# Two small moves in a long-convolution kernel: which engine copies part of Z out of PSUM, and which queue reads an identity matrix

## The chip, the cores and the metric

The kernel runs on one core of one Trainium2 chip. A core has five engines that run their own instruction streams side by side: TensorE (PE in the profile; its weight loads are listed apart as PEld), VectorE (DVE), ScalarE (ACT), GpSimd (POOL) and SyncE (SP), which only issues transfers here. They wait for each other through semaphores. The metric is device time in microseconds; the time shown is the median of three runs.

## The reference

The input x is 8 batches of 5696 positions and 128 channels. Two steps follow each other. The first is a causal convolution of each channel with a filter h as long as the sequence, done with transforms of twice the length:

```python
Xf = np.fft.rfft(x, n=L, axis=1)          # L = 2 * 5696
Hf = np.fft.rfft(h, n=L, axis=0)
y = np.fft.irfft(Xf * Hf[None], n=L, axis=1)[:, :S, :]
```

The second takes the lowest 64 frequencies of that result, mixes the channels of each with a complex 128x128 matrix, transforms back, adds, and ends with one matrix product:

```python
X = np.fft.rfft(y, axis=1)[:, :64]
Y = complex product of X with w_r + i w_i, mode by mode
u = y + np.fft.irfft(Y padded with zeros, n=S, axis=1)
out = u + np.maximum(u @ w_ch, 0.0)
```

## The kernel before, in words

The batches go in four pairs (`g_` from 0 to `NP - 1` = 3). The sequence is split as 89 x 64, and each transform becomes matrix products in float16. For each pair the kernel first makes the tiles `As` (a transform over the 89), and then runs through 90 frequencies `k` in 23 ticks of four (`ticks`, `KT = 4`), followed by three ticks in which the pipeline empties. The function `tick(g_, t)` writes out one such step, and the order in which it emits instructions is the order on every engine: each engine has one queue, and a recorder adds the semaphore waits that the data need. Helpers issue almost everything, so the profile shows their lines: 323 for a matmul, 311 for a ScalarE copy, 315 for a VectorE copy, 320 for a transfer.

In the last three pairs a tick consists of:

- `second(g_, t)`: 32 matmuls in two ticks (`ps<-As,M`), emitted for t and t + 1 together when t is odd;
- `products(g_, t, ...)`: the product with the filter's spectrum, on VectorE (`U<-Xs,Hs`, line 637). In three ticks of four ScalarE first copies the matmuls' result from PSUM to the tile `Xs`, and VectorE reads that copy. In each tick with t % 4 == 3 (`straight`) VectorE reads PSUM itself (`U<-ps,Hs`);
- for the tick `s_ = t - 2` (`LC = 2`): four matmuls with the matrices W1 and W2 (`ps<-U,Wc`), two for each batch b of the pair, and after each two a copy of the bank to the tile Z (`Zs` or `Zt`, half b). Both copies are on ScalarE. Three PSUM banks take turns for this (`ZBANK`). A transfer on SP's queue then writes Z to DRAM (`zscr<-Zs`);
- for the tick `s_ = t - 3` (`LM = 3`): eight matmuls that read Z as their weights (`ps<-G,Zs`), for each of the four frequencies first b = 0, then b = 1. They gather the 64 low modes.

So on TensorE the order in an odd tick is `As,M`, `U,Wc`, `G,Z`, and in the even tick after it `U,Wc`, `G,Z`. The `G,Z` matmuls of a tick read the Z that was copied in the tick before. On VectorE the order is one product a tick.

In the last pair the list `early` has, at certain ticks, transfers and clearings for the stage that follows: weights, tables, the first chunks of Z read back (`load_zt`) and zeros in 32 rows of them, by GpSimd (`clear_zt`). At tick 14 it calls `load_id()`, `load_ib()` and `clear_zt(1)` in that order. `load_id` reads a 128x128 identity, which is used once, in the eight transposes of Y (line 824) after the pair. Its tile lies where the Z tiles 8 and 9 were, so the transfer waits until those have been read and written out (`ZY`).

After the last pair come the mode mixing, the transposes of Y, and the long last stage, in which 16 chunks of Z are read back and each output tile is made of matmuls, one ScalarE and one VectorE pass and a transfer.

Of the kernel before, what the change touches and what calls it, by code (L numbers as in the profile page):

```python
# [4 lines left out]
P = 128  # L5
# [118 lines left out]
def bass_long_conv_fft__then__afno_spectral_mix_kernel(nc, x, h, moe_w_r, moe_w_i, moe_w_ch, out):  # L124
    B, S, D = x.shape
# [7 lines left out]
    NP = B // 2  # L133
# [17 lines left out]
    c, s = np.cos(th), np.sin(th)  # L151
# [35 lines left out]
    def const(name, a):  # L187
        return nc.inline_tensor(np.ascontiguousarray(a.astype(np.float16)), name=name)
# [3 lines left out]
    c_w = const("cW", np.concatenate([w1, w2, np.eye(P)], axis=1))  # L192
# [5 lines left out]
    zs = nc.dram_tensor("zscr", [NP * NK * P, 2 * D], F16, kind="Internal")  # L198
# [7 lines left out]
    def at(name, cols, dt, off):  # L206
        return nc.alloc_sbuf_tensor_at(name, [P, cols], dt, offset=off)
# [75 lines left out]
    id_sb = at("Id", P, F16, r_off[1])  # L283
# [8 lines left out]
    def pv(bank, off, dims, p0=0, n=P):  # L292
        return bass.AP(ps, p0 * 4096 + bank * 512 + off, [[4096, n]] + [list(d) for d in dims])
# [5 lines left out]
    def bank(i):  # L299
        return ("bank", i)  # L300
# [18 lines left out]
    def dma(eng, dst, src, ring, reads=(), writes=(), after=()):  # L319
        R.add(eng, lambda h_: h_.dma_start(dst, src), reads, writes, ring=ring, after=after)  # L320
# [14 lines left out]
    def turns(name, items):  # L335
        i = ring2.get(name, 0)
        ring2[name] = i + 1
        return items[i % len(items)]
# [25 lines left out]
    def x_place(i, src, toks):  # L364
        R.add("vector", lambda e: e.tensor_copy(bass.AP(x_sb, i * XN * XS, [[XW, NQ], [XS, XN], [1, D]]),  # L365
                                                src),
              list(toks) + XZ, [("xin", i)])
# [72 lines left out]
    for j in range(16):  # L440
        t = turns("h", [0, 2, 4])
# [5 lines left out]
        for i in range(4 if j < 15 else 26):  # L447
# [4 lines left out]
             eng="vector" if j in (3, 7) else "scalar")  # L452
# [25 lines left out]
    def xtok(n):  # L478
        return [("xt", n, p_) for p_ in range(2)]

    def x_room(g_, i):
        if g_ > 1:
            return x_st[i]
        return x_h[i] if i < NXH else x_st[i - NXH]
# [37 lines left out]
    ZY = [("zs", i, b) for i in range(NZL, NZX) for b in range(2)]  # L522
# [42 lines left out]
    pace = []  # L565

    def load_id():
        dma("sync", id_sb[:, :], bass.AP(c_w, 2 * P, [[3 * P, P], [1, P]]), "c", (), [("id",)], after=ZY)

    def load_wi():  # L570
        dma("gpsimd", wi_sb[:, P:2 * P], bass.AP(c_w, 2 * P, [[3 * P, P], [1, P]]), "p", (), [("i16",)], after=M_ALL[5:6])
# [6 lines left out]
    LC, LM, LH = 2, 3, 6  # L578
# [3 lines left out]
    def with_h_at(g_, t):  # L582
        return g_ == 0 and t + LH < NT
# [10 lines left out]
    def twin(g_, t):  # L594
        return g_ > 0 and t % 2 == 1
# [4 lines left out]
    def slot_of(g_, t):  # L600
        if g_ == 0 or t == 0:
            return XSLOT[(t + 1) % 2 if t and not with_h_at(g_, t) else 0]
        return XSLOT[((t - 1) // 4 + t) % 2]

    def second(g_, t):
        sl = slot_of(g_, t)
        for i, k in enumerate(ticks[t]):
            for r in range(2):
                for b in range(2):
                    col = k * 3 * J + (J if r == 0 else 0) + b * J  # L610
                    mm(pv(sl + b, i * D, [[1, D]]),
                       ap(m_sb, MW, J * b, J, col, [[1, P]]),
                       ap(a_sb, AW, J * b, J, (2 * k + r) * D, [[1, D]]), r == 0, r == 1,
                       AST + mtok(k), [bank(sl + b)])

    def products(g_, t, sl):
        n = len(ticks[t])
        bk = [bank(sl), bank(sl + 1)]
        i = t % NU
        hv = bass.AP(h_sb, KT * t * D, [[2 * HW, P], [HW, 2], [0, 2], [1, n * D]])  # L620
        uv = bass.AP(u_s[i], 0, [[2048, P], [1024, 2], [512, 2], [1, n * D]])
        src = pv(sl, 0, [[0, 2], [512, 2], [1, n * D]])
        if t == 0:
            e = turns("e", list(range(NXS)))
            evac(bass.AP(x_s[e], 512, [[1024, P], [1, n * D]]), pv(sl + 1, 0, [[1, n * D]]), [bank(sl + 1)], [("xs", e)], eng="scalar")
            hv = bass.AP(h_sb, 0, [[2 * HW, P], [HW, 2], [1, n * D]])
            for b, s_, tok in ((0, pv(sl, 0, [[0, 2], [1, n * D]]), bank(sl)),
                               (1, bass.AP(x_s[e], 512, [[1024, P], [0, 2], [1, n * D]]), ("xs", e))):
                R.add("vector", lambda e, b=b, s_=s_: e.tensor_tensor(bass.AP(u_s[i], b * 512, [[2048, P], [1024, 2], [1, n * D]]), s_, hv, MULT),  # L629
                      [tok, ("h", t, 0), ("h", t, 1, 0), ("h", t, 1, J)], [("u", i)])  # L630
            return
        if not straight(g_, t):
            e = onchip.get((g_, t))
            if e is None:
                e = copied(g_, t, sl)
            src, bk = bass.AP(x_s[e], 0, [[1024, P], [0, 2], [512, 2], [1, n * D]]), [("xs", e)]
        R.add("vector", lambda e: e.tensor_tensor(uv, src, hv, MULT),  # L637
              bk + [("h", t, 0), ("h", t, 1, 0), ("h", t, 1, J)], [("u", i)])
# [10 lines left out]
    def tick(g_, t):  # L649
        if g_ + 1 < NP:  # L650
            for i in range(2 * XC):
                if t == XPLACE[g_ > 0][i]:
                    x_place(i, bass.AP(x_room(g_ + 1, i), 0, [[XB, NQ], [D, XN], [1, D]]), xtok(i))
        with_h = with_h_at(g_, t)
        if t < NT:
            of_two = t > 0 and twin(g_, t - 1)
            if not of_two:
                second(g_, t)
            products(g_, t, slot_of(g_, t))
            if twin(g_, t):  # L660
                second(g_, t + 1)
                if straight(g_, t):
                    copied(g_, t + 1, slot_of(g_, t + 1))
        drain = list(border[t]) if t in border and g_ + 1 < NP else []
        if drain and t >= NT:
            j, sl, e = drain.pop(0)
            a_tile(j, [sl], e)
        if g_ + 1 < NP:
            i = t // 2 - 1 if t % 2 == 0 else -1
            if g_ == 0:  # L670
                i = XLATE.index(t) + NXH if t in XLATE else -1
            if 0 <= i < 2 * XC:
                x_load(g_ + 1, i, x_room(g_ + 1, i), xtok(i), [("u", t % NU)] + AST)
        if LC <= t < NT + LC:
            s_ = t - LC
            n = len(ticks[s_])
            i, zi = s_ % NU, zroom(g_, s_)
            zb = [turns("z", ZBANK) for b in range(2)]
            for b in range(2):
                for r in range(2):  # L680
                    mm(pv(zb[b], 0, [[1, n * D]]), (W1, W2)[r], u_s[i][:, r * 1024 + b * 512:r * 1024 + b * 512 + n * D],
                       r == 0, r == 1, [("u", i), ("wc",)], [bank(zb[b])])
                evac(bass.AP(z_s[zi], b * D, [[1024, P], [2 * D, n], [1, D]]),
                     pv(zb[b], 0, [[D, n], [1, D]]), [bank(zb[b])], [("zs", zi, b)], eng="scalar",
                     after=once(("zx", zi, b), Z_OLD) if zi >= NZ else ())
            zo = (g_ * NK + KT * s_) * P * 256
            dma("sync", bass.AP(zs, zo, [[256, P], [P * 256, n], [1, 256]]),
                bass.AP(z_s[zi], 0, [[1024, P], [256, n], [1, 256]]), "z",
                [("zs", zi, 0), ("zs", zi, 1)], [("zd", g_, s_)])
            if drain and t >= NT:  # L690
                j, sl, e = drain.pop(0)
                a_tile(j, [sl], e)
        if LM <= t < NT + LM:
            s_ = t - LM
            zi = zroom(g_, s_)
            for i, k in sorted(enumerate(ticks[s_]), key=lambda q: (s_ > 0 or q[1] != 1, q)):
                for b in range(2):
                    if k % 2:
                        o, off, n, sl = pv(MB, b * P, [[1, P]]), (k + 1) // 2 * P, P, (k + 1) // 2
                    else:  # L700
                        ms, off = even[k]
                        n, sl = 2 * len(ms), 0
                        dims = [[M, 2]] if len(ms) == 1 else [[ms[1] - ms[0], 2], [M, 2]]
                        o = pv(MB, b * P + ms[0], dims)
                    mm(o, z_s[zi][:, i * 256 + b * P:i * 256 + b * P + P], g_sb[:, off:off + n],
                       k == 1 and b == 0, k == NK - 1 and b == 1, [("g", sl // GP), ("zs", zi, b)], [bank(MB)])
        if drain and t < NT + LM - 1:
            j, sl, e = drain.pop(0)
            a_tile(j, [sl], e)
        if with_h:  # L710
            filter_tick(t + LH, [2, 3])
# [106 lines left out]
    for hb in range(2):  # L818
        evac(bass.AP(y_sb, hb * 32 * B, [[2 * M * B, P], [B, 32], [M * B, 2], [1, B]]),
             pv(6 + hb, 0, [[2 * B, 32], [B, 2], [1, B]]), [bank(6 + hb)], [("y", hb)], eng="vector" if hb else "scalar",  # L820
             after=ZY)
# [117 lines left out]
```

## Time and profile before

| | us |
|---|---|
| median of three runs | 382.4 (381.59 to 383.15) |
| the profiled execution, whole | 381.7 |
| its span, first to last instruction | 379.9 |
| TensorE busy in the span | 359.7 |
| ScalarE busy | 314.4 |
| VectorE busy | 294.9 |
| GpSimd busy | 75.1 |
| mean granted TensorE clock | 0.989 |

The profiled execution has 1.8 us outside its span. The ticks of the last pair lie between 217 and 258 us of the span. A row of the timeline gives the start, the duration, the engine and the operation of one instruction or of several of the same kind; the brackets give the idle time before it and the event that ended it. On VectorE and ScalarE an instruction may start a little before the one ahead of it has ended, so start to start is shorter than the duration.

### The profile page before, as it was taken

How to read it: one execution, taken by the hardware profiler on the slowest of the kernel's cores; microseconds unless marked ns; L12 is line 12 of the kernel's file. 1: busy time of each engine (PE TensorE's matmuls, PEld its weight loads, DVE VectorE, ACT ScalarE, POOL GpSimd, SP SyncE). 2: the span in 40 equal slices, each digit the busy share in tenths (PEclk: the TensorE clock that was granted, in tenths of full speed). 3: DMA queues.
4: the chain of work that ended last, by engine and by line, in shares of the span. 5: the costliest groups of instructions: out<-in, count | busy, mean ns of one | idle time of the engine just before them, and what ended most of it. 6: DMA issues, size and time to landing. Idle time of an engine off the chain costs nothing.

```text
span 379.9 us, 12434 instructions
## 1 busy us (share of the span) xinstructions
PE 359.7 (95%) x5346; PEld 278.9 (73%) x5346; DVE 294.9 (78%) x333; ACT 314.4 (83%) x495; POOL 75.1 (20%) x117
## 2 busy tenths in 40 slices
PE   7889899999989999989999999999999999999994
PEld 7778766666856666856667856668889889988873
DVE  3649799878988999989998888882437767766666
ACT  8469689898989997989997999995457776788884
POOL 8713012100642220733310301124000000000000
PEclk9999999999999999999999999998899999999999
DMA  7999959979799997999995989999999999999878
GB/s 149 206 292 362 248 147 231 236 205 267 87 143 202 238 250 217 103 125 212 259 253 168 95 302 364 372 360 383 372 390 376 374 412 404 418 405 382 319 296 320
DMA packets 87048, 103.94 MB, mean 274 GB/s; under 512 B 22730, under 2 KB 72522, under 8 KB 83438
## 3 DMA queue, kind: packets, MB, share of 16 engines
q1 hardware_dynamic: 64610, 81.33, 60.7%
q0 software_dynamic: 22384, 21.83, 34.8%
q8 instruction: 42, 0.69, 0.7%
q14 instruction: 12, 0.10, 0.1%
HBM read 70.61 MB, written 51.12 MB: 320 GB/s over the span
## 4 chain that ended last, share of the span: by engine, by line
PE 66%; ACT 13%; DVE 7%; DMA 6%; issue 4%; POOL 3%; DVEq 0%; ACTq 0%; POOLq 0%
PE ps L323 65%; ACT As L313 7%; DMA Xr<-in_x_dram 4%; DVE As L317 2%; ACT Zs L311 2%; DMA zscr<-Zs 2%; DVE U L629 2%; ACT Zt L311 2%; POOL Xr L320 2%; ACT Xs L311 1%; DVE Xin L365 1%; ACT R L871 1%; POOL Hin L320 1%; DVE U L637 1%; DVE Hs L315 1%
## 5 line engine op out<-in xcount | busy, mean ns | idle before, releaser
L637 DVE TENSOR_TENSOR U<-Xs,Hs 128x2048 f16<-128x2048 f16 (+1 forms) x73 | 86.9, 1192 | 14.3 <-ACT Xs L311 11.3
L323 PE MATMUL ps<-U,Wc 128*128 128x512 f16 (+1 forms) x368 | 94.2, 376 | 0.5 <-DVE U L629 0.5
L311 ACT CAST Xs<-ps 128x1024 f16<-128x1024 f32 (+1 forms) x77 | 75.0, 978 | 12.3 <-PE ps L323 7.3
L311 ACT CAST Zs<-ps 128x512 f16<-128x512 f32 (+1 forms) x132 | 69.2, 594 | 2.0 <-PE ps L323 1.7
L872 DVE TENSOR_TENSOR O<-ps,R 128x512 f32<-128x512 f32 x81 | 52.3, 684 | 20.1 <-ACT R L871 11.2
L317 DVE TENSOR_SCALAR As<-ps 128x720 f16<-128x720 f32 (+1 forms) x67 | 55.6, 880 | 5.7 <-PE ps L323 4.0
L871 ACT ACTIVATE R<-ps 128x512 f32<-128x512 f32 (+1 forms) x92 | 50.5, 591 | 8.5 <-PE ps L323 8.4
L323 PE MATMUL ps<-F,Xin 128*128 128x180 f16 x512 | 52.4, 250 | 3.7 <-DVE Xin L365 2.2
L323 PE MATMUL ps<-As,M 64*128 64x128 f16 x1440 | 50.3, 217 | 3.8 <-DVE U L629 3.0
L323 PEld LDWEIGHTS ps<-F,Xin 128*128 128x128 f16 x512 | 44.5, 155 | 11.1 <-DVE As L317 3.2
L313 ACT ACTIVATE As<-ps 128x720 f16<-128x720 f32 (+1 forms) x65 | 45.8, 768 | 7.2 <-PE ps L323 6.6
L323 PE MATMUL ps<-WI,UT 128*128 128x256 f16 x360 | 51.1, 278 | 0.5 <-ACT UT L311 0.4
L311 ACT CAST UT<-ps 128x712 f16<-128x712 f32 x46 | 34.5, 752 | 19.2 <-PE ps L323 18.0
L323 PEld LDWEIGHTS ps<-U,Wc 128*128 128x128 f16 x368 | 28.6, 97 | 29.7 <-ACT Zs L311 3.8
L323 PEld LDWEIGHTS ps<-As,M 64*128 64x128 f16 x1440 | 40.5, 94 | 10.0 <-DVE U L629 3.7
L323 PEld LDWEIGHTS ps<-WI,UT 128*128 128x128 f16 x360 | 39.0, 152 | 3.4 <-issue 1.8
L323 PE MATMUL ps<-IBs,C 128*128 128x356 f16 x128 | 40.3, 325 | 0.1
L320 POOL DMA_DIRECT2D Xt<-in_x_dram x40 | 21.5, 541 | 81.2 <-PE ps L323 80.7
L323 PEld LDWEIGHTS ps<-G,Zs 128*128 128x128 f16 x512 | 26.1, 96 | 14.5 <-ACT Zs L311 2.0
L637 DVE TENSOR_TENSOR U<-ps,Hs 128x2048 f16<-128x2048 f32 x15 | 34.3, 2284 | 0.0
L323 PE MATMUL ps<-G,Zs 128*128 128x128 f16 (+2 forms) x512 | 32.2, 192 | 0.1
L311 ACT CAST Zt<-ps 128x512 f16<-128x512 f32 x52 | 28.5, 622 | 0.2 <-PE ps L323 0.2
(74 smaller groups left out, 489.0 us busy)
## 6 DMA issues: line engine op xcount, KB each, us to landing
out_dram<-O SPq DMA_DIRECT2D x39, 512.0 KB, 6.9
zscr<-Zs SPq DMA_DIRECT2D x62, 256.0 KB, 6.8
zscr<-Zt SPq DMA_DIRECT2D x26, 256.0 KB, 6.7
Xt<-in_x_dram POOLq DMA_DIRECT2D x20, 320.0 KB, 7.3
W<-wscr SPq DMA_DIRECT2D x4, 1024.0 KB, 7.0
ZT0a<-zscr SPq DMA_DIRECT2D x4, 1024.0 KB, 8.2
M<-cM POOLq DMA_DIRECT2D x5, 720.0 KB, 17.0
ZT1a<-zscr SPq DMA_DIRECT2D x3, 1024.0 KB, 8.3
```

The costliest lines, as they stand in the source:

```text
L311: R.add(e, lambda h_: h_.copy(dst, src), reads, writes, after=after)
L313: R.add(e, lambda h_: h_.activation(dst, src, COPY, scale=scale), reads, writes, after=after)
L315: R.add(e, lambda h_: h_.tensor_copy(dst, src), reads, writes, after=after)
L317: R.add(e, lambda h_: h_.tensor_scalar_mul(dst, src, scale), reads, writes, after=after)
L320: R.add(eng, lambda h_: h_.dma_start(dst, src), reads, writes, ring=ring, after=after)
L323: R.add("tensor", lambda h_: h_.matmul(o, l, r, start=st, stop=sp), reads, writes)
L365: R.add("vector", lambda e: e.tensor_copy(bass.AP(x_sb, i * XN * XS, [[XW, NQ], [XS, XN], [1, D]]), src), list(toks) + XZ, [("xin", i)])
L629: R.add("vector", lambda e, b=b, s_=s_: e.tensor_tensor(bass.AP(u_s[i], b * 512, [[2048, P], [1024, 2], [1, n * D]]), s_, hv, MULT), [tok, ...
L637: R.add("vector", lambda e: e.tensor_tensor(uv, src, hv, MULT), bk + [("h", t, 0), ("h", t, 1, 0), ("h", t, 1, J)], [("u", i)])
L871: R.add("scalar", lambda e: e.activation(rv, src_r, RELU), bk, [("r", i % NR)], after=once(("r", i % NR), G_ALL + XTT + [("y", 0), ("y", 1 ...
L872: R.add("vector", lambda e: e.tensor_tensor(ov, src_u, rv, ADD), bk + [("r", i % NR)], [key + (h_,)], after=once(key, old))
```

## The change

In the last pair, in the ticks 5, 9, 13, 17 and 21 (t % 4 == 1, t above 3), the copy of Z's second half (b = 1) is done by VectorE instead of ScalarE. In these ticks VectorE's queue then has the product of tick t, the copy of Z for tick t - 2, and the product of tick t + 1. And the identity is read on GpSimd's queue instead of SP's, with semaphores of the ring `q` instead of `c`; on GpSimd it stands after the clearing of the first chunk and ahead of the clearing of the second.

```diff
     def load_id():
-        dma("sync", id_sb[:, :], bass.AP(c_w, 2 * P, [[3 * P, P], [1, P]]), "c", (), [("id",)], after=ZY)
+        dma("gpsimd", id_sb[:, :], bass.AP(c_w, 2 * P, [[3 * P, P], [1, P]]), "q", (), [("id",)], after=ZY)
...
                 evac(bass.AP(z_s[zi], b * D, [[1024, P], [2 * D, n], [1, D]]),
-                     pv(zb[b], 0, [[D, n], [1, D]]), [bank(zb[b])], [("zs", zi, b)], eng="scalar",
+                     pv(zb[b], 0, [[D, n], [1, D]]), [bank(zb[b])], [("zs", zi, b)],
+                     eng="vector" if g_ == NP - 1 and t % 4 == 1 and b == 1 and t > LC + 1 else "scalar",
                      after=once(("zx", zi, b), Z_OLD) if zi >= NZ else ())
```

## The prediction

> **What bounds the kernel now.** I read the page's busy times first, then the chain that ended last, then the windows for the stage that the change touches, and there the timeline of each engine. The page:
>
> ```profile
> PE 359.7 (95%) x5346; PEld 278.9 (73%) x5346; DVE 294.9 (78%) x333; ACT 314.4 (83%) x495; POOL 75.1 (20%) x117
> ```
>
> TensorE is the fullest engine, but these are means over unlike stages. The chain through the last pair's ticks is this:
>
> ```profile
> 219.75 33.33 PE ps L323 x524
> ```
>
> From 219.75 to 253.08 it never leaves TensorE. Four full periods of four ticks lie between 224.28 and 252.44; the windows view gives them (us, busy time of PE, PEld, DVE, ACT, POOL, clock):
>
> ```profile
> 224.28:252.44 28.16, 28.16 (x452) 18.27 (x450) 22.99 (x16) 27.59 (x46) 3.59 (x2) 1.00 1.03 337
> ```
>
> TensorE is busy for all 28.16 us, 7.04 a period; ScalarE for 27.59, VectorE for 22.99. So TensorE sets the pace with ScalarE close behind, and whatever delays one matmul here is lost for good. One of the changed places, tick 5 and the start of tick 6, engine by engine:
>
> ```profile
> 224.28 1.07 PE L323 MATMUL ps<-As,M 64*128 64x128 f16 x32
> 225.28 1.04 PE L323 MATMUL ps<-U,Wc 128*128 128x512 f16 x4
> 226.15 0.49 PE L323 MATMUL ps<-G,Zs 128*128 128x2 f16 x8
> 226.48 1.02 PE L323 MATMUL ps<-U,Wc 128*128 128x512 f16 x4
> 227.34 0.49 PE L323 MATMUL ps<-G,Zs 128*128 128x2 f16 x8
> ...
> 224.94 1.01 ACT L311 CAST Xs<-ps 128x1024 f16<-128x1024 f32 x1
> 225.92 1.07 ACT L311 CAST Zs<-ps 128x512 f16<-128x512 f32 x2
> 226.88 1.03 ACT L311 CAST Xs<-ps 128x1024 f16<-128x1024 f32 x1
> ...
> 226.05 1.23 DVE L637 TENSOR_TENSOR U<-Xs,Hs 128x2048 f16<-128x2048 f16 x1 [0.67 <-ACT Xs L311]
> 228.01 1.23 DVE L637 TENSOR_TENSOR U<-Xs,Hs 128x2048 f16<-128x2048 f16 x1 [0.73 <-ACT Xs L311]
> 229.15 2.28 DVE L637 TENSOR_TENSOR U<-ps,Hs 128x2048 f16<-128x2048 f32 x1
> ```
>
> The two ScalarE copies (225.92, x2) are Z of tick 3: b = 0 from 225.92, b = 1 done by 226.99. The reader of both is the row of eight G matmuls at 227.34; its second matmul, some 0.03 later, is the first that needs b = 1. So ScalarE's copy has 0.38 to spare. VectorE works on the product of tick 5 until 227.28 and then waits 0.73 for ScalarE.
>
> **The copies, part by part.** Five copies leave ScalarE. Each takes it 0.48 from start to start (four Z copies in a row span 2.06, the last lasting about 0.6). That is worth to TensorE only what it waits for ScalarE. In the steady ticks this is small: in each period one U,Wc matmul comes 0.03 late, after a Z copy that frees its bank (copy 229.78 to 230.37, matmul at 230.42, where 230.39 was due). Four such waits come behind a moved copy: 0.12. At the end of the pair there is more: one row of four U,Wc matmuls takes 1.13 where the steady rows take 1.04, and twelve G matmuls take 1.10 where eight take 0.49 and four more would make about 0.67: 0.09 + 0.43 = 0.52. So 0.64 is all that ScalarE's relief can give.
>
> VectorE's copy is not in the trace for Z; the nearest row is its cast of Y, the same shape, types and source:
>
> ```profile
> 264.12 0.69 DVE L315 CAST Y<-ps 128x512 f16<-128x512 f32 x1 [3.07 <-PE ps L323]
> ```
>
> I take 0.69, as nothing but the destination's stride differs; from below ScalarE's 0.59 for the same copy, from above 0.90, VectorE's cast of 712 columns. By width the copy fits VectorE's idle 0.73. What counts is when it ends. It stands behind the product of tick 5. That product cannot start before 226.05, since its Xs ends at 225.95, whose copy began when the As,M matmuls of tick 5 were done: this is tied to TensorE, not to ScalarE's load. Behind such a product the next instruction starts 1.14 later (228.01 to 229.15), so the copy runs from 227.19 to 227.88. From a copy's end to the waiting matmul it takes 0.05 (230.37 to 230.42), so the second G matmul starts at 227.93 instead of 227.37: TensorE, which runs in order, stands for 0.57. With a copy of 0.59 it would be 0.47, with 0.90 it would be 0.78.
>
> The same sum at the other places, from the start of the product to the second G matmul: tick 9, 233.09 + 1.14 + 0.69 + 0.05 = 234.97 against 234.40, 0.57; tick 13, 242.01 against 241.44, 0.57; tick 17, 249.40 against 248.48, 0.92, because its product starts 0.35 later than in the other ticks for a reason that the trace does not settle (0.57 if that goes); tick 21, 256.09 against 255.30, 0.79, because it has only 24 As,M matmuls ahead of it. Together 3.1 to 3.4. Each tick's start is tied to TensorE, so a later place finds the same distance, and nothing is caught up.
>
> From this go the 0.12 above. Of the 0.52 at the end, about 0.15 go: following the last copies there one by one, with ScalarE one copy (0.48) ahead and TensorE 0.79 behind, two waits for Z of 0.11 and 0.24 remain. The sum: 3.25 - 0.12 - 0.15 = 3.0 later. With the bounds of the copy (5 x 0.10 less, 5 x 0.21 more) it is 2.5 to 4.1.
>
> What is queued behind the copy on VectorE is the product of tick 6. It moves from 228.01 to 227.80 (copy to next start about 0.61), since ScalarE, freed of one copy, has its Xs ready at 227.41 instead of 227.91. Its reader, U,Wc of tick 8, starts at 229.96, so it costs nothing; without that cover a late product would cost up to 0.61 a place. SP's write of Z waits for VectorE too, 0.9 later, with a load of weights behind it that is first used at 259.37: 30 us of cover.
>
> **The identity.** On SP it is issued when the write of Z tile 9 has landed, and everything on SP stands behind it until then:
>
> ```profile
> 245.78 0.33 SPq L320 DMA_DIRECT2D Id<-cW  x1
> ```
>
> It lands 4.4 later, at 250.2, and is used at 264.91. On GpSimd it goes out at about the same time, takes 0.57 to issue and 5.6 to land as the other small read on that queue does (WI): 252, still 13 us early; past that, every microsecond would count in full. Behind it on GpSimd the clearing of ZT1b, now at 243.43, moves to some 246.4 and ends near 248.2; TensorE reads that chunk from 269.72. On SP the table IBs, two writes of Z and chunk ZT1 are no longer held up to 245.78; no engine waits for one of them, so this gives nothing. All of this is 0.
>
> **Sum.** 381.7 + 3.0 = 384.7 for the profiled execution. It lies 0.7 below the median, so against the median it is 385.4. Behind the pair the chain stays on TensorE for 90 us, so the 3.0 reaches the end.
>
> **What can shift it: the clock.** In the windows view TensorE's clock is halved for 6.83 us after the pair:
>
> ```profile
> 262.27:269.10 6.83, 6.60 (x99) 5.41 (x97) 2.79 (x4) 2.05 (x4) 0.00 (x0) 0.50 1.03 363
> 269.10:275.93 6.83, 6.83 (x128) 6.05 (x127) 2.70 (x3) 2.62 (x5) 0.00 (x0) 1.00 1.01 385
> ```
>
> The mixing matmuls (until 263.9) keep their pace in it; behind them a matmul of 356 columns steps by 0.30 instead of 0.15, one of 89 by 0.075 instead of 0.043, a transpose by 0.107, where a matmul of 128 columns steps by 0.055. Seven, sixteen and eight of these: 1.0 + 0.5 + 0.4 = 1.9 lost. If it comes at the same time while the work is 3.0 later, it covers more mixing and loses 0.9 to 1.0: the kernel is then at 384.4. If it falls wholly on dense work it loses 3.4: 386.9. [...]
>
> **Rivals.**
> - Not slower: the copy is hidden and ScalarE's relief remains. For it: VectorE's idle 0.73 is wider than 0.69. Against it: it decides at 227.37, so the product would have to start 0.57 earlier, and it starts 0.10 after its Xs. Price: -0.64 at best, 381.8. Over 0.5% faster has no source that I can find.
> - VectorE becomes the bound: the copy makes the products late too, and each place costs another 0.61: 382.4 + 3.0 + 3.05 = 388.5. Against it: VectorE is busy for 22.99 of 28.16, and four copies add 2.4.
> - The stalls come, but the halved clock falls on other work: 384.4 or 386.9, above.
>
> **How the numbers follow.** Stalls as summed, clock as it was: 0.50 (385.4, from 384.9 to 386.5 by the copy's bounds). Stalls with a cheaper halved stretch: 0.20. With a dearer one: 0.12. Copy hidden: 0.10. VectorE the bound: 0.08. About 0.5% is what a measurement of this kernel can tell from no change: 1.9 us. The first three cases make 0.82. The range goes from 384.4 less the runs' own scatter of 0.8 to 386.9. Slower by over 0.5% means above 384.3: the first, third and fifth case and nearly half of the second, 0.78; within 0.5%: 0.20; faster: 0.02.
>
> **What would show it.** Right: in the profile after, the second G matmul of ticks 6, 10, 14, 18 and 22 starts 0.5 to 0.9 behind the first, released by VectorE's Z copy; the period is about 7.6 instead of 7.04; ScalarE's share there falls to about nine tenths; the identity lands by 253 and nothing waits for it. Wrong: no such gap (a copy that starts ahead of 226.6), products late at U,Wc, or a stall at the transposes.

## The result and the profile after

The changed kernel takes 384.9 us (median of six runs, 383.6 to 385.5), the kernel before in the same six rounds 381.7. The ratio is 1.0078 with a 95% interval from 1.0054 to 1.0103: 3.0 us slower by the ratio (the two medians differ by 3.2), where 3.0 had been summed. The profiled execution took 384.6, 2.9 above the one of before. The page's line of busy times hardly differs:

```profile
PE 360.5 (94%) x5346; PEld 279.1 (73%) x5346; DVE 297.8 (78%) x338; ACT 312.2 (82%) x490; POOL 76.3 (20%) x118
```

The five copies are there (DVE x338 against x333, ACT x490 against x495). Where the time went is told by the windows view of the same four periods (us, then busy time of PE, PEld, DVE, ACT, POOL, the clock):

```profile
223.88:254.38 30.50, 28.78 (x452) 18.22 (x450) 26.08 (x21) 25.73 (x42) 4.73 (x4) 1.00 1.04 322
```

The same 452 matmuls take 30.50 instead of 28.16, 7.62 a period instead of 7.04. ScalarE went from 27.59 to 25.73, from 98% of the stretch to 84%, and these periods gained nothing by it. The timeline of ticks 5 and 6 shows the place; first TensorE, then ScalarE, then VectorE:

```profile
223.88 1.07 PE L323 MATMUL ps<-As,M 64*128 64x128 f16 x32
224.88 1.04 PE L323 MATMUL ps<-U,Wc 128*128 128x512 f16 x4
225.75 0.49 PE L323 MATMUL ps<-G,Zs 128*128 128x2 f16 x8
226.08 1.02 PE L323 MATMUL ps<-U,Wc 128*128 128x512 f16 x4
226.94 0.17 PE L323 MATMUL ps<-G,Zs 128*128 128x2 f16 x1
227.54 0.47 PE L323 MATMUL ps<-G,Zs 128*128 128x2 f16 x7 [0.43 <-DVE Zs L315]
...
225.52 0.59 ACT L311 CAST Zs<-ps 128x512 f16<-128x512 f32 x1
226.00 1.02 ACT L311 CAST Xs<-ps 128x1024 f16<-128x1024 f32 x1
229.05 1.01 ACT L311 CAST Xs<-ps 128x1024 f16<-128x1024 f32 x1 [1.05 <-PE ps L323]
...
225.66 1.22 DVE L637 TENSOR_TENSOR U<-Xs,Hs 128x2048 f16<-128x2048 f16 x1 [0.67 <-ACT Xs L311]
226.80 0.68 DVE L315 CAST Zs<-ps 128x512 f16<-128x512 f32 x1
227.40 1.21 DVE L637 TENSOR_TENSOR U<-Xs,Hs 128x2048 f16<-128x2048 f16 x1
```

The row of eight G matmuls is torn: one runs at 226.94, the other seven from 227.54, released by VectorE's copy, which started behind the product and ended at 227.48. Without a wait the second one starts 0.03 behind the first, so the gap is 0.57. The product of tick 6 starts at 227.40, right behind the copy. The view of waits gives the five places together, as loads of weights and as matmuls that waited (us in all, how often, the longest):

```profile
PEld ps L323 <- DVE Zs L315: 3.1, 4, 0.9
PE ps L323 <- DVE Zs L315: 1.9, 4, 0.7
PEld ps L323 <- DVE Zt L315: 0.7, 1, 0.7
PE ps L323 <- DVE Zt L315: 0.4, 1, 0.4
```

None of these lines is in the kernel before. (Idle time counts from a matmul's modelled end, so it is less than the gap from start to start.) And the chain that ended last, which ran through TensorE alone here before, now has VectorE's copy in each period (start, us):

```profile
242.05 0.69 DVE Zs L315
242.74 0.05 issue
242.79 4.60 PE ps L323 x79
247.41 1.02 ACT Xs L311
```

The chain names the rest of the argument too: the copy releases TensorE, TensorE's matmuls release the Xs copy on ScalarE, that releases the product, and the product stands ahead of the next copy.

For all kernels below I use one measure beside the time: the stretch from the start of the last pair's first U,Wc matmul to the start of the first S4a matmul behind the pair. It is 219.75 to 258.29 = 38.55 us before and 219.35 to 260.80 = 41.45 after: 2.91 longer.

### The profile page after: what moved, and what is told of

Same layout as the page of the kernel before. It is cut to its first block, busy times and chain, and to the rows that moved or that the text cites. A ratio compares the mean times of both kernels' runs of the same rounds, so it can differ in the third digit from the quotient of the medians.

```text
span 382.7 us, 12437 instructions
## 1 busy us (share of the span) xinstructions
PE 360.5 (94%) x5346; PEld 279.1 (73%) x5346; DVE 297.8 (78%) x338; ACT 312.2 (82%) x490; POOL 76.3 (20%) x118
## 4 chain that ended last, share of the span: by engine, by line
PE 60%; ACT 12%; DMA 10%; DVE 9%; issue 4%; POOL 3%; SPq 0%; DVEq 0%; ACTq 0%; POOLq 0%
PE ps L323 59%; ACT As L313 6%; DMA Xr<-in_x_dram 4%; DVE As L317 2%; ACT Xs L311 2%; DVE U L637 2%; DMA zscr<-Zs 2%; DMA Xt<-in_x_dram 2%; DMA Hs<-Hs 2%; DVE U L629 2%; POOL Xr L320 2%; ACT Zs L311 1%; ACT Zt L311 1%; DVE Xin L365 1%; POOL Hin L320 1%
## 5 line engine op out<-in xcount | busy, mean ns | idle before, releaser
L311 ACT CAST Zs<-ps 128x512 f16<-128x512 f32 (+1 forms) x128 | 67.3, 592 | 3.0 <-PE ps L323 2.8
```

The source lines that it names most:

```text
L311: R.add(e, lambda h_: h_.copy(dst, src), reads, writes, after=after)
```

## The experiments

**Each part alone.** The first leaves `load_id` as it was, the second leaves the copies.

```diff
# copies only, against the changed kernel
-        dma("gpsimd", id_sb[:, :], ..., "q", (), [("id",)], after=ZY)
+        dma("sync", id_sb[:, :], ..., "c", (), [("id",)], after=ZY)
# identity only, against the kernel before
-        dma("sync", id_sb[:, :], ..., "c", (), [("id",)], after=ZY)
+        dma("gpsimd", id_sb[:, :], ..., "q", (), [("id",)], after=ZY)
```

> Only the five Z copies go to VectorE; the identity stays on SP's queue. Theory (the copy stands behind the tick's product on VectorE and ends 0.57 after the second G matmul is due): the whole loss is here, 2.9 us (+-1.0 for the halved clock stretch) over the kernel before; five gaps of about 0.60, 0.60, 0.60, 0.60, 0.82 between the first and second G matmul, and 41.4 to 41.5 us from the last pair's first U,Wc matmul to the first S4a matmul (before 38.55, after 41.45). Rival (the identity on GpSimd's queue costs a good part): clearly less than 2 us over before.

> Only the identity moves to GpSimd's queue; all Z copies stay on ScalarE. Theory: no change, within 1 us of before, the pair's stretch 38.5 to 38.6 us, the identity landed by 256 and the transposes not waiting for it. Rival (the queue move costs): 0.5 us or more over before with a new wait at GpSimd's clearing or at the transposes.

| | median us | before, same rounds | ratio (95%) | stretch us |
|---|---|---|---|---|
| changed kernel | 384.91 | 381.68 | 1.0078 (1.0054 to 1.0103) | 41.45 |
| copies only | 384.39 | 381.96 | 1.0053 (1.0026 to 1.0080) | 41.46 |
| identity only | 381.63 | 381.96 | 0.9992 (0.9971 to 1.0012) | 38.54 |

The copies have the whole loss: their stretch is that of the changed kernel within 0.01, and the two ratios' intervals overlap. The identity's queue changes nothing that can be measured, and the stretch with it alone is that of before. What differs between 384.39 and 384.91 is not in the stretch.

**The same copies, ahead of the product.** VectorE does the same work, in another order, in four of the five places.

```diff
+        first_copy = g_ == NP - 1 and t % 4 == 1 and LC + 1 < t < NT - 2
...
-            products(g_, t, slot_of(g_, t))
+            if first_copy:
+                copied(g_, t, slot_of(g_, t))
+            else:
+                products(g_, t, slot_of(g_, t))
...
-                     eng="vector" if g_ == NP - 1 and t % 4 == 1 and b == 1 and t > LC + 1 else "scalar",
+                     eng="vector" if first_copy and b == 1 else "scalar",
...
+            if first_copy:
+                products(g_, t, slot_of(g_, t))
             zo = (g_ * NK + KT * s_) * P * 256
```

> As the changed kernel, but in the ticks 5, 9, 13 and 17 VectorE's copy of Z stands ahead of the product of the same tick instead of behind it (tick 21 keeps its copy on ScalarE). VectorE does the same work in these ticks. Theory (the order on VectorE is the cause): the copy runs from about 0.05 after its matmuls to 0.3 ahead of the G matmul that reads it, the product moves 0.9 later and still is in time for its U,Wc matmuls; no gap over 0.1 at G, pair's stretch 38.2 to 38.6, the time within 0.7 us of before. Rival (VectorE has no room for the copies, its load is the cause): 1.5 us or more over before, gaps moved to U,Wc or As,M.

The ratio is 1.0008 (0.9986 to 1.0030), and the stretch 38.55, to the hundredth that of before. VectorE and TensorE in tick 5 and 6 of this kernel (timeline):

```profile
228.31 0.69 DVE L315 CAST Zs<-ps 128x512 f16<-128x512 f32 x1 [0.97 <-PE ps L323]
228.91 2.35 DVE L637 TENSOR_TENSOR U<-Xs,Hs 128x2048 f16<-128x2048 f16 x2
231.18 2.28 DVE L637 TENSOR_TENSOR U<-ps,Hs 128x2048 f16<-128x2048 f32 x1
...
227.23 1.04 PE L323 MATMUL ps<-U,Wc 128*128 128x512 f16 x4
228.10 0.49 PE L323 MATMUL ps<-G,Zs 128*128 128x2 f16 x8
228.43 1.03 PE L323 MATMUL ps<-U,Wc 128*128 128x512 f16 x4
229.29 0.49 PE L323 MATMUL ps<-G,Zs 128*128 128x2 f16 x8
```

The copy ends at 229.00, the row of G matmuls starts at 229.29 and stays whole. The product is later, and nobody waits for it. So VectorE has the room; the order was the cause. The run also tells what the change could have gained in the steady ticks: four copies are off ScalarE here and nobody waits for VectorE, and still the stretch is not shorter. (The median, 382.92, is 0.96 above that of before. The profiled execution of this kernel has an extra stretch at half clock in the first stage; the last section comes back to both.)

**The same order, a later reader.** The changed kernel, with the last pair's G matmuls four ticks behind.

```diff
-        if LM <= t < NT + LM:
-            s_ = t - LM
+        lm = LM + (g_ == NP - 1)
+        if lm <= t < NT + lm:
+            s_ = t - lm
...
-        for t in range(NT + LM):
+        for t in range(NT + LM + (g_ == NP - 1)):
```

> The changed kernel with one edit: in the last pair the G matmuls run four ticks behind instead of three, so they read a Z copied two ticks earlier. VectorE's order and its five copies stay as in the changed kernel. Theory: the copies are no less late, but nobody waits for them; the gaps at G go, the pair's stretch is 38.0 to 38.6 us, the time 0.0 to 0.6 below before. Rival (the copies hurt through VectorE's load or through the later writes of Z on SP): 1.5 us or more over before remain.

The ratio is 0.9991 (0.9973 to 1.0009): the loss is gone, with all five late copies in place. The stretch, 38.66, is a little over what I had expected, for two waits that I had not seen coming. At the pair's start TensorE has no G matmuls for a tick longer, and there one U,Wc matmul waits 0.36 for a Z copy of ScalarE. And the copy of tick 21 is so late that its other user waits for it, the U,Wc matmul that needs its PSUM bank (timeline of TensorE):

```profile
254.82 0.49 PE L323 MATMUL ps<-G,Zs 128*128 128x4 f16 x8
255.64 1.04 PE L323 MATMUL ps<-U,Wc 128*128 128x512 f16 x4 [0.34 <-DVE Zs L315]
```

That is the next wait behind the first one, 0.50 from start to start over the usual step.

**The later reader alone**, the same edit on the kernel before, for what it is worth by itself.

> The kernel before (all copies on ScalarE, the identity on SP) with the G matmuls of the last pair four ticks behind instead of three. Theory: the waits of 0.5 at the end of the pair shrink and nothing else changes, pair's stretch 38.0 to 38.5 us, the time 0 to 0.5 under before, too little for the measurement to tell. Rival: the copies on VectorE, not the later reader, set the time of the late-reader run, and this one comes out more than 0.5 us faster or slower than that.

The ratio is 1.0004 (0.9982 to 1.0025) and the stretch 38.38, 0.17 shorter than before: of 0.52 of waits at the pair's end 0.23 remain, and the 0.36 at the start is new. That alone would make the stretch 0.07 longer. But six rows of G matmuls, one in four ticks, last 0.52 instead of 0.49 in the kernel before, because their copies come a little late; with the later reader all of them last 0.49, and one U,Wc wait of 0.03 is gone too. It is the shortest stretch of all, and too small a gain for the times to show.

**Other places for the five copies, and fewer of them.** Only the condition changes.

```diff
-                     eng="vector" if g_ == NP - 1 and t % 4 == 1 and b == 1 and t > LC + 1 else "scalar",
# even ticks
+                     eng="vector" if g_ == NP - 1 and t % 4 == 0 and b == 1 and LC + 1 < t < NT else "scalar",
# two copies
+                     eng="vector" if g_ == NP - 1 and t in (5, 13) and b == 1 else "scalar",
# behind the long product
+                     eng="vector" if g_ == NP - 1 and t % 4 == 3 and b == 1 and LC + 1 < t < NT else "scalar",
```

> The changed kernel with VectorE's copies in the ticks 4, 8, 12, 16 and 20 (t % 4 == 0) instead of 5, 9, 13, 17 and 21: again five copies, each again behind its tick's product. Theory (what costs is when the copy ends against its reader): after the product of tick 8 (232.48) the copy would end at 233.17 and its reader is due at 233.22, so the gaps at G are 0.05 or less, at tick 20 about 0.25; pair's stretch 38.5 to 38.9 us, the time within 0.8 us of before. Rival (five copies are too much for VectorE): 2 us or more over before, as in the changed kernel.

> The changed kernel with VectorE's copy in the ticks 5 and 13 alone. Theory: two gaps of 0.57 each at G and no others, pair's stretch 38.55 + 1.14 = 39.7 us. Rival (the loss is a start-up or a one-time effect): a stretch near 38.5 or near 41.4.

> The changed kernel with VectorE's copies in the ticks 7, 11, 15 and 19 (t % 4 == 3), behind the products that read PSUM and take 2.28. Theory, by the same sum: start of that product 229.15 + 2.20 + 0.69 + 0.05 = 232.09 against a G matmul due at 230.91, so 1.18 at each of four places, 4.7 us over before, though there is one copy less than in the changed kernel; pair's stretch 43.2 us. Rival (each copy costs a fixed price of about 0.6): 2.3 us.

| copies in ticks | gaps at G, us (start to start, over the usual step) | stretch us | ratio (95%) |
|---|---|---|---|
| 4, 8, 12, 16, 20 | 0.21 at tick 20 alone | 38.59 | 1.0006 (0.9983 to 1.0029) |
| 5, 13 | 0.57, 0.57 | 39.72 | one execution: 382.7 us |
| 5, 9, 13, 17, 21 (the change) | 0.57, 0.57, 0.57, 0.57, 0.79 | 41.45 | 1.0078 (1.0054 to 1.0103) |
| 7, 11, 15, 19 | 1.20, 1.20, 1.20, 1.20 | 43.28 | 1.0139 (1.0094 to 1.0184) |

Five copies cost next to nothing in the even ticks (0.21 at tick 20, of which 0.17 comes back at the pair's end, where ScalarE has less to do), and four cost 1.20 each behind the product that reads PSUM. That kernel's TensorE and VectorE (timeline):

```profile
230.08 0.17 PE L323 MATMUL ps<-G,Zs 128*128 128x2 f16 x1
231.31 0.47 PE L323 MATMUL ps<-G,Zs 128*128 128x2 f16 x7 [1.06 <-DVE Zs L315]
...
228.37 2.28 DVE L637 TENSOR_TENSOR U<-ps,Hs 128x2048 f16<-128x2048 f32 x1
230.57 0.68 DVE L315 CAST Zs<-ps 128x512 f16<-128x512 f32 x1
```

In the even ticks the copy ends a hair ahead of the matmul that reads it (VectorE's copy of tick 8, then TensorE in tick 9, of that kernel):

```profile
232.95 0.68 DVE L315 CAST Zt<-ps 128x512 f16<-128x512 f32 x1
233.55 1.22 DVE L637 TENSOR_TENSOR U<-Xs,Hs 128x2048 f16<-128x2048 f16 x1
...
232.78 1.04 PE L323 MATMUL ps<-U,Wc 128*128 128x512 f16 x4
233.65 0.51 PE L323 MATMUL ps<-G,Zt 128*128 128x2 f16 x8
```

The copy ends at 233.63 and the row of G starts at 233.65; its 0.51 instead of 0.49 is all that is seen. So the price of a copy is neither per copy nor for VectorE's load. It is the time by which the copy's end misses its reader, and it can be read from the profile of before. The products of ticks 7, 8 and 9 there, and the rows of G matmuls that would wait for a copy behind the first two (timeline of VectorE, then TensorE):

```profile
229.15 2.28 DVE L637 TENSOR_TENSOR U<-ps,Hs 128x2048 f16<-128x2048 f32 x1
231.35 1.21 DVE L637 TENSOR_TENSOR U<-Xs,Hs 128x2048 f16<-128x2048 f16 x1
233.09 1.23 DVE L637 TENSOR_TENSOR U<-Xs,Hs 128x2048 f16<-128x2048 f16 x1 [0.53 <-ACT Xs L311]
...
230.86 0.52 PE L323 MATMUL ps<-G,Zs 128*128 128x2 f16 x8
233.19 0.49 PE L323 MATMUL ps<-G,Zt 128*128 128x2 f16 x8
```

For tick 8 that is 231.35 + 1.13 + 0.69 + 0.05 = 233.22 against a second G matmul at 233.22. So the sum gives 0.00 for the ticks 8, 12 and 16, 0.57 for the ticks 5, 9 and 13 and 1.18 behind the long product; measured were 0.02 at most, 0.57 and 1.20. VectorE's idle time behind the product does not tell this: 0.53 in tick 8, where a copy of 0.68 was hidden, and 0.73 in tick 5, where it was not.

## Why the prediction was right, and where it was not

- **The stall.** Forecast: the second G matmul 0.57 late at three places, 0.57 to 0.92 at tick 17, 0.79 at tick 21. Measured: 0.570, 0.572, 0.573, 0.569 and 0.793. The lateness of 0.35 of tick 17's product, which I had left open, did not come again in the changed kernel, so the sum was 3.08 and not 3.25.
- **The duration of VectorE's copy**, taken from its cast of Y at 0.69, was 0.68.
- **Wrong: "Four such waits come behind a moved copy: 0.12."** None of them went. The changed kernel has the same step of 0.25 instead of 0.216 between two U,Wc matmuls once in each period (251, 250, 252 and 251 ns in the four periods that follow a copy). I had put these waits down to ScalarE's load. But ScalarE stood idle for 1.05 ahead of the Xs copy at 229.05 (its row is above): that copy waits for TensorE's own As,M matmuls, and the Z copy that frees the bank comes after it. The Xs copy starts 1.11 behind the start of the As,M row in both kernels (227.76 to 228.87 before, 227.94 to 229.05 after). It is a chain from TensorE through two ScalarE copies back to TensorE, and a lighter ScalarE does not shorten it: the same step of 0.25 stands in the kernels with the copies ahead of the product and in the even ticks.
- **The end of the pair.** Forecast: 0.15 of 0.52 go, with waits of 0.11 and 0.24 left. Measured: 0.11 and 0.21 left, so 0.20 go.
- **The sum.** 3.25 - 0.12 - 0.15 = 3.0 forecast. Measured: 3.08 - 0.20 = 2.88 by the gaps, 2.91 by the stretch. The misses, 0.17 too much on one side and 0.07 too much on the other, partly cancel, so that the 3.0 came so close is in part luck. The profiled execution is 2.87 slower as a whole; on the way it gained 0.40 ahead of the pair, before any changed instruction, and lost about as much in the stretch at half clock, by where that fell against the work. The forecast of 385.4 stood on a median of 382.4 for the kernel before, which was 381.7 in the six rounds; with it the sum gives 384.7, and 384.9 was measured. ScalarE's share of the four periods fell further than the "about nine tenths" of the forecast, to 84%: the stall makes the periods longer, and ScalarE stands idle in it too.
- **The rivals.** VectorE as the bound falls: its products were in time in the changed kernel, and with the copy ahead of the product everything fits. That the copy might be hidden was right about the room (0.73 for 0.68) and wrong about when the room comes; put elsewhere it is hidden.
- **The identity.** Nothing waited for it, as forecast, but it came later than I had said: issued at 249.13, landed 6.5 later, at 255.6, where I had 252 and "by 253", a sign of being right that did not come. GpSimd's queue in the changed kernel (timeline):

```profile
249.13 0.57 POOL L320 DMA_DIRECT2D Id<-cW  x1 [12.78 <-PE ps L323]
249.69 1.82 POOL L536 MEMSET ZT1b<- 32x2048 uint32 x1
```

  The transfer waits for the write of Z tile 9, whose last part landed at 248.57 in this execution, against 245.76 before and 244.92 with the identity alone. Why it landed later stays open. Of the cover 11.7 us were left, and the clearing behind it ended 21 us ahead of its first use.
- **The clock.** I had held it possible that the half-clock stretch stays where it is in time while the work moves past it. It does not. Before it was 262.27 to 269.10, beginning 2.90 behind the first mixing matmul (259.37); in the changed kernel it is 265.76 to 272.58, beginning 3.88 behind that matmul (261.88). In the ten profiles it begins 2.1 to 3.9 us behind it, though that matmul moves from 258.7 to 263.3 between them. The windows view of the changed kernel:

```profile
265.76:272.58 6.82, 6.59 (x76) 5.16 (x73) 2.78 (x4) 2.00 (x3) 0.00 (x0) 0.50 1.05 381
```

  So the stretch follows the work, but not by the same amount: the first mixing matmul came 2.5 later and the stretch 3.5 later. What sets its place these profiles do not show. From the transposes' start to the first ZT1a matmul, where most of what it slows lies, it took 4.81 before (264.91 to 269.72) and 5.28 in the changed kernel (267.34 to 272.62); the ten profiles have 4.1 to 5.3. The two other cases for the clock, 384.4 and 386.9, were estimates, and neither came: the stretch cost about 0.5 more than before, where they had 0.9 to 1.0 less and 1.5 more.

## What to carry to other kernels

An engine with idle time can take over work for free only if the work ends there before its reader is due. So look up three starts in the timeline: the instruction ahead of it on the new engine, what that one is tied to, and the reader; here this gave 0.00, 0.57 and 1.18 us for three kinds of place, and they came out within 0.02, save tick 17, where the product ahead started earlier than in the profile of before. How long the engine is idle did not tell them apart. Relief of an engine at 98% was worth nothing here in the steady ticks, since what it waits for there is the bound engine's own output; look at whether its wait would end earlier, not at how full it is. And if a piece must be late, give it an earlier place in its queue or a later reader before giving up the idea: both took the whole loss away.

## What was not expected of the hardware

Two of the ten profiles have a second stretch at half clock in the first stage; the other eight have a granted clock of 1.00 from 20 to 40 us. This is the windows view of the kernel with the copy ahead of the product:

```profile
28.50:32.00 3.50, 3.43 (x25) 3.26 (x24) 2.50 (x4) 2.63 (x4) 3.34 (x7) 0.53 1.02 423
32.00:40.00 8.00, 7.84 (x141) 6.59 (x140) 7.25 (x10) 7.34 (x12) 0.00 (x0) 0.99 1.05 303
```

The other one is the later reader alone, with a clock of 0.52 from 28.50 to 32.00 and 1.00 on both sides. From these means I estimate about 3.4 us at half clock in each. In these two the first U,Wc matmul of the first pair starts at 49.8 and 49.5 us, in the other eight at 48.1 to 48.6, and they are the two profiled executions, 383.6 and 383.3 us, that are longer than their stretch explains. All these kernels are the same up to the last pair, so it is chance, 0.8 to 1.6 us at a time. The single runs have no profile, but the mean granted clock of each is on record, and it fits this. The profiles of these two kernels have a mean of 0.985 where the other eight have 0.988 to 0.990, and 3.4 us more at half clock in 380 lower the mean by 0.0045. Of the 47 runs of the kernel before that were taken beside the experiments, 8 have a mean of 0.984 or 0.985 and take 383.3 us on average; the other 39, at 0.988 to 0.992, take 381.8. Of the ten runs of the kernel with the copy ahead of the product five have 0.984 or 0.985; the median of the other five is 382.0. So its median of 382.92 says nothing against the order of the copies. What sets off the early stretch stays open.
